# Token rows scattered straight into their expert's slot, without a token table, and two short static pieces

## The chip, the core and the metric

The kernel runs on one core of one Trainium2 chip. The metric is the device time of one execution, in microseconds (us); lower is better. Engines are called as in the profile: PE (TensorE, matmuls), DVE (VectorE), ACT (ScalarE), POOL (GpSimd), SP (SyncE, which here mostly issues DMAs). A q after the name (SPq) is the engine's own queue.

## The reference

A decayed linear attention ("retention") over 4 batches, 8 heads, 768 positions and head size 64 gives 3072 tokens of 512 features. They go through a mixture of 8 experts of which each token uses one:

```python
state = gamma * state + k[t] (x) v[t]            # per batch and head, 64 x 64
y[t]  = scale * q[t] @ state
x     = y as 3072 tokens x 512
logits = x @ w_gate + modality_bias[modality_id] # 8 experts
e_idx  = argmax(logits); gate_w = softmax(logits)[e_idx]
for e in range(8):                               # tokens whose e_idx is e
    out[mask] = gate_w[mask] * (relu(x[mask] @ w1[e]) @ w2[e])   # 512 -> 1024 -> 512
```

## The kernel before, in words

**Retention.** 24 tiles of 128 tokens (`NN`), six per batch. `retention(n)` is one tile, written as four steps with a `yield` behind each: state update (`state`, L200), scores of the next tile (`scores`, L139), projection of the previous tile (`tokens_out`, L180) and output heads (`heads_out`, L157). Loads run ahead on SP: keys and queries three tiles (`load_kq`, four buffers), values and token-wise keys two. `decay_v` (L130, POOL) scales the values; `decay_q` (L123, POOL) makes, once at the start, the six scaled versions of the table `dcq`, from which `heads_out` takes that of its tile. `tokens_out` multiplies by identity and gate weights in one matmul, so that a row of `xs` holds four groups of 128 features and 8 partial logits (`XW` = 544 floats, 2176 bytes); ACT copies it out of PSUM and stores it at the token's own place in `x_dram` (L190).

**Routing.** After every three tiles (a group, `GRP`) `route_a` finds the expert and the gate of 384 tokens and `route_b` the position: expert times 3072 plus the running number within the expert. `scatter` (L333) then writes, per tile, one row of 8 bytes per token (token number and gate) to that position of the table `tbl`, by an indirect DMA of POOL.

**Jobs.** A slot is 512 positions of one expert (`SLOT`); 48 slots could exist (`NCAND`). A job computes one slot: `ids_in` (L520, SP) reads the slot's 512 table rows, `gather` (L529) fetches their token rows from `x_dram` by four indirect DMAs of POOL, `flip` (L556) transposes them on PE and splits them into a high and a low part (ACT and DVE), `raw` and `cut` load the expert's weights and split them likewise, `first` and `second` are 96 matmuls each, and the result is scaled by the gate (ACT, L599) and scattered to `out` (POOL, L600). A job has 32 steps of 6 matmuls (`job_steps`); `hooks_of(k)` hangs work for the job itself and loads, transposes and cuts for the next one on these steps (a hook at q runs ahead of step 2q).

Two early jobs (`EARLY`: after groups 3 and 5) take a full slot each while retention goes on: from tile 14 on (`FIRST_JOB`), the steps of retention are put between job steps, two and one in turn. `early_a` to `early_e` choose the early slots. When all tokens are routed, `final_a` to `final_c` rank the slots left by size; four more jobs (`NLAST`) are laid out statically for the first four of them. SP reads slot and expert of each from a small list (`place`, `reg`). Where exactly five slots are left and the fifth has at most `TAIL` = 32 tokens, it goes through a short piece (`rest_in` to `rest_second`, L643 to L715), whose work is laid among the last two static jobs; otherwise the piece runs on the empty slot. All further slots go through a dynamic loop (L910), one pass each, which begins with loads and has no work of a neighbour to cover them.

**What sets the order.** PE, ACT, DVE and SP run in the order in which the program emits (`manual_schedule`); on POOL the pinned instructions keep it. `at(n, where, ...)` puts a piece of routing at a place of tile n: `top`, `st` (behind the state update), `sc` (behind the scores), `pr` (ahead of the projection), `tk` (behind it), `end`. Waits between engines come from the tiles' and DRAM tensors' uses; `disjoint` declares that scatters to other rows don't wait for each other.

Of the kernel before, what the change touches and what calls it, by code (L numbers as in the profile page):

```python
# [15 lines left out]
P = 128  # L16
# [4 lines left out]
NG = H // 2  # L21
# [12 lines left out]
TROWS = (NCAND + 1) * SLOT  # L34
# [9 lines left out]
C_ID, C_MASK, C_DEC, C_IOTA, C_GRP, C_FAC, C_END = 0, 128, 256, 304, 312, 313, 337  # L44
# [3 lines left out]
def kernel(  # L48
# [29 lines left out]
    x_dram = dr.tile([NT + P, XW], F32, name="x_dram")  # L78
    tbl = dr.tile([TROWS, 2], I32, name="tbl")
# [3 lines left out]
    dcq = cp.tile([P, NCH, NG, P], F32, name="dcq")  # L83
# [3 lines left out]
    fac = cst[:, C_FAC : C_FAC + NCH * NG].rearrange("p (c g) -> p c g", g=NG)  # L87
    iota_e = cst[:, C_IOTA : C_IOTA + NE]
# [6 lines left out]
    rows = cp.tile([P, NN, 2], I32, name="rows")  # L95
# [8 lines left out]
    kqs, kts, vts, vds, lg, mid = {}, {}, {}, {}, {}, {}  # L104
# [18 lines left out]
    def decay_q(c):  # L123
        pin(
            nc.gpsimd.tensor_tensor(
                dcq[:, c], dcq[:, 0], fac[:, c].unsqueeze(2).to_broadcast([P, NG, P]), op=ALU.mult
            )
        )
# [28 lines left out]
    def heads_out(n, a, vd, qv, s):  # L157
# [17 lines left out]
        for j in range(2):  # L175
            b = slice(2 * j, 2 * j + 2)
            nc.vector.tensor_tensor(yT[:, b], py[j], dcq[:, n % NCH, b], op=ALU.mult)  # L177
        return yT

    def tokens_out(n, yT):  # L180
        xs = wk.tile([P, NG, P + NE], F32, tag="xs", name=f"xs_{n}", bufs=3)
        for u in range(2):
# [7 lines left out]
        nc.scalar.dma_start(  # L190
            x_dram[n * P : (n + 1) * P, :].rearrange("t (g e) -> t g e", g=NG), xs
        )
        gr = n // GRP
        if n % GRP == 0:
            lg[gr] = sm.tile([P, GRP, NE], F32, tag="lg", name=f"lg_{gr}")
# [16 lines left out]


# [14 lines left out]
    def setup_rows():  # L228
        pin(nc.gpsimd.iota(rows[:, :, 0:1], [[P, NN], [0, 1]], base=0, channel_multiplier=1))
        fill["sent"] = me.tile([P, QW], F32, tag="raw", name="sent", bufs=4)  # L230
        sent = fill["sent"].bitcast(I32)[:, : TROWS // P * 2].rearrange("p (r w) -> p r w", w=2)
        pin(nc.gpsimd.memset(sent, 0))
        pin(nc.gpsimd.memset(sent[:, :, 0:1], NT))
        fill["zer"] = me.tile([P, QW], F32, tag="raw", name="zer", bufs=4)
        pin(nc.gpsimd.memset(fill["zer"][:, :XW], 0.0))

    def setup_stores():
        sent = fill["sent"].bitcast(I32)[:, : TROWS // P * 2].rearrange("p (r w) -> p r w", w=2)
        nc.sync.dma_start(tbl.rearrange("(p r) w -> p r w", p=P), sent)
        nc.sync.dma_start(x_dram[NT : NT + P, :], fill["zer"][:, :XW])  # L240

    def setup_room():
        jobs[0].xg = rows_room(jobs[0])
        for t in jobs[0].xg:
            pin(nc.gpsimd.memset(t, 0.0))
# [34 lines left out]
    def route_a(gr, part):  # L280
# [24 lines left out]
        else:  # L305
# [4 lines left out]
            nc.vector.reciprocal(rows.bitcast(F32)[:, tk, 1], den)  # L310
# [22 lines left out]
    def scatter(gr, which=range(GRP)):  # L333
        pos = mid[gr]
        for i in which:
            ins = nc.gpsimd.indirect_dma_start(  # L336
                out=tbl[:, :],
                out_offset=bass.IndirectOffsetOnAxis(ap=pos[:, i : i + 1], axis=0),
                in_=rows[:, gr * GRP + i, :],
                in_offset=None,  # L340
                bounds_check=NCAND * SLOT - 1,
# [676 lines left out]
```

## Time and profile before

| | us |
|---|---|
| median of 3 runs | 571.94 |
| lowest and highest run | 569.14, 573.87 |
| the profiled execution's own time | 571.58 |
| its span, first to last instruction | 569.8 |
| PE busy (matmul) | 497.5, 87% |
| DVE, ACT, POOL busy | 226.8, 166.7, 126.8 |
| DMA | 85.39 MB, mean 150 GB/s |

How to read it: the page cuts the span into 40 equal slices of 14.2 us and gives each engine's busy share in tenths (9 is 90% or more), the clock granted to PE in tenths of full speed, and the mean busy share of the 16 DMA engines with what they moved. A timeline row has start, duration, engine, line, operation, output <- inputs, count, and in square brackets how long the engine stood idle before it and what released it. A row of stretches has the stretch, its length, busy time and instruction count of PE, PEld (weight loads), DVE, ACT and POOL, then the granted clock, the DMA share and GB/s. A row of groups has busy time, mean duration in ns, and the idle time in front.

### The profile page before, as it was taken

Reading aid. Unit: us, or ns where it says so; the run is one execution under the profiler, and the core shown is the slowest. Engines: PE = TensorE matmul, PEld = TensorE weight load, DVE = VectorE, ACT = ScalarE, POOL = GpSimd, SP = SyncE. Lnnn points to the kernel's source line nnn. Section 1 sums busy time; section 2 is a strip of 40 time slices with the busy share of each in tenths; the row PEclk is TensorE's granted clock in tenths of the full one; section 3 lists DMA queues with packets and bytes.
Section 4 is the critical chain, followed back from the end, with each engine's and each line's share of the span. In section 5 each row is a group of like instructions: output and inputs, shape, how many; then the busy total and the mean of one; then the engine's idle time right before and its main releaser. Section 6 shows DMA issues by size and latency. Waiting matters only on the chain. (4 is left out here: it accounts for less than half of the span.)

```text
span 569.8 us, 8974 instructions
## 1 busy us (share of the span) xinstructions
PE 497.5 (87%) x3420; PEld 407.3 (71%) x3420; DVE 226.8 (40%) x460; ACT 166.7 (29%) x273; POOL 126.8 (22%) x132
## 2 busy tenths in 40 slices
PE   5997751999999999999999999999994799618995
PEld 5875640877887778888888888887883588506884
DVE  2764540776664455324425513622402440024400
ACT  1221120433332324334433424423313431024210
POOL 3553303222431322112022012120014100130011
PEclk9998785998999999999999999999998699956998
DMA  8989787296984436335335354862213500074000
GB/s 296 282 260 272 139 248 257 73 281 110 347 192 126 82 119 194 135 114 187 130 129 169 114 179 160 315 209 91 75 54 106 168 3 1 3 239 134 0 0 1
DMA packets 32838, 85.39 MB, mean 150 GB/s; under 512 B 7309, under 2 KB 7565, under 8 KB 32800
## 3 DMA queue, kind: packets, MB, share of 16 engines
q1 hardware_dynamic: 23104, 62.45, 37.2%
q0 software_dynamic: 5952, 15.31, 8.2%
q10 hardware_dynamic: 3744, 7.12, 3.4%
q8 instruction: 25, 0.41, 0.3%
q14 instruction: 13, 0.11, 0.1%
HBM read 71.38 MB, written 15.64 MB: 153 GB/s over the span
## 5 line engine op out<-in xcount | busy, mean ns | idle before, releaser
L553 DVE TENSOR_TENSOR lo_f<-raw_f,hi_f 128x1024 fp32r<-128x1024 f32 x32 | 39.2, 1225 | 49.3 <-ACT hi_f L551 44.5
L592 PE MATMUL o_f<-hi_f,hTh_f 128*128 128x512 f32 x128 | 50.5, 394 | 0.0
L574 PE MATMUL h_f<-xTh_f,hi_f 128*128 128x512 f32 x128 | 50.2, 393 | 0.0
L592 PE MATMUL o_f<-lo_f,hTh_f 128*128 128x512 f32 x128 | 49.9, 390 | 0.0
L592 PE MATMUL o_f<-hi_f,hTl_f 128*128 128x512 f32 x128 | 49.9, 390 | 0.0
L574 PE MATMUL h_f<-xTh_f,lo_f 128*128 128x512 f32 x128 | 49.9, 389 | 0.0
L574 PE MATMUL h_f<-xTl_f,hi_f 128*128 128x512 f32 x128 | 49.9, 389 | 0.0
L582 DVE SCALAR_TENSOR_TENSOR hTl_f<-h_f,hTh_f 128x512 fp32r<-128x512 f32 x32 | 21.9, 690 | 56.2 <-ACT hTh_f L581 54.2
L553 DVE TENSOR_TENSOR lo_dyn<-raw_dyn,hi_dyn 128x1024 fp32r<-128x1024 f32 x16 | 19.0, 1221 | 58.9 <-ACT hi_dyn L551 58.9
L151 DVE TENSOR_TENSOR a<-sc,cst 128x512 f32<-128x512 f32 x48 | 30.9, 684 | 27.5 <-PE sc L146 22.7
L600 POOL DMA_INDIRECT out_dram<-o_f,ids_f x16 | 15.8, 987 | 107.3 <-ACT o_f L599 96.1
L134 POOL TENSOR_TENSOR vd<-vt,cst 128x512 f32<-128x512 f32 x24 | 25.1, 1045 | 60.9 <-DMA vt<-in_qkv_dram 19.5
L146 PE MATMUL sc<-kq 64*128 64x128 f32 x384 | 32.9, 315 | 5.6 <-DMA kq<-in_qkv_dram 5.1
L559 PE MATMUL xp_dyn<-cst,xg_dyn 128*128 128x128 f32 x32 | 8.6, 432 | 31.0 <-DMA xg_dyn<-x_dram,ids_dyn 30.9
L146 PEld LDWEIGHTS sc<-kq 64*128 64x128 f32 x384 | 27.6, 215 | 10.2 <-DMA kq<-in_qkv_dram 5.3
L581 ACT ACTIVATE hTh_f<-h_f 128x512 fp32r<-128x512 f32 x32 | 19.1, 598 | 53.6 <-PE h_f L574 52.4
L551 ACT CAST hi_f<-raw_f 128x1024 fp32r<-128x1024 f32 x32 | 33.4, 1043 | 0.0
L336 POOL DMA_INDIRECT tbl<-rows,pos x24 | 24.6, 1026 | 36.0 <-DVE pos L330 14.5
L189 ACT COPY xs<-x 128x272 f32<-128x272 f32 x48 | 18.2, 385 | 48.9 <-PE x L185 38.2
L600 POOL DMA_INDIRECT out_dram<-o_dyn,ids_dyn x8 | 7.9, 990 | 101.0 <-ACT o_dyn L599 101.0
L185 PE MATMUL x<-wgt,yT 128*128 128x136 f32 x192 | 29.8, 301 | 0.5 <-DVE yT L177 0.5
L559 PEld LDWEIGHTS xp_dyn<-cst,xg_dyn 128*128 128x128 f32 x32 | 5.7, 217 | 33.9 <-DMA xg_dyn<-x_dram,ids_dyn 33.8
(192 smaller groups left out, 1052.9 us busy)
## 6 DMA issues: line engine op xcount, KB each, us to landing
raw_f<-in_w_dram SPq DMA_DIRECT2D x32, 512.0 KB
kq<-in_qkv_dram SPq DMA_DIRECT2D x23, 512.0 KB
raw_e<-in_w_dram SPq DMA_DIRECT2D x16, 512.0 KB
raw_dyn<-in_w_dram SPq DMA_DIRECT2D x16, 512.0 KB
x_dram<-xs ACTq DMA_DIRECT2D x24, 272.0 KB
vt<-in_qkv_dram SPq DMA_DIRECT2D x24, 256.0 KB
kt<-in_qkv_dram SPq DMA_DIRECT2D x20, 256.0 KB
rw<-in_w_dram SPq DMA_DIRECT2D x6, 512.0 KB
```

Of the source, the lines that this page charges most:

```text
L134: nc.gpsimd.tensor_tensor(vds[n], vv, dec[:, n % NCH].unsqueeze(2).to_broadcast([P, H, D]), op=ALU.mult)
L146: nc.tensor.matmul(pe[j][:, g * P : (g + 1) * P], kt[r, g], qt[r, g], start=True, stop=True, skip_group_check=True,)
L151: nc.vector.tensor_tensor(a[:, j], pe[j].rearrange("p (h t) -> p h t", t=P), mask.unsqueeze(1).to_broadcast([P, NG, P]), op=ALU.mult,)
L185: nc.tensor.matmul(px[:, g], yT[:, 2 * u + g], wgt[:, 2 * u + g], start=(g == 0), stop=(g == 1), skip_group_check=True,)
L336: ins = nc.gpsimd.indirect_dma_start(out=tbl[:, :], out_offset=bass.IndirectOffsetOnAxis(ap=pos[:, i : i + 1], axis=0), in_=rows[:, gr * G ...
L551: nc.scalar.copy(hi, t)
L553: nc.vector.tensor_tensor(lo, t, hi.bitcast(F32), op=ALU.subtract)
L574: nc.tensor.matmul(s.ph, s.w[1][f // 2][wi][:, o : o + P], s.xT[kc][a], start=(kc == 0 and k == 0), stop=(kc == KC - 1 and k == 2),)
L581: nc.scalar.activation(hi, s.ph, AF.Relu)
L582: nc.vector.scalar_tensor_tensor(lo, s.ph, 0.0, hi.bitcast(F32), op0=ALU.max, op1=ALU.subtract)
L592: nc.tensor.matmul(s.po, s.hT[f][a][:, hh * P : (hh + 1) * P], s.w[2][f // 2][wi][:, (f % 2) * DM : (f % 2 + 1) * DM], start=(f == 0 and k ...
L600: ins = nc.gpsimd.indirect_dma_start(out=out[:, :], out_offset=bass.IndirectOffsetOnAxis(ap=s.ids[:, hh, 0:1], axis=0), in_=o[:, :], in_of ...
```

## The change

Rows go straight to their place. `x_dram` and `tbl` are gone; `xsl` (8 experts x 3072 rows and one empty slot, 2176 bytes a row) takes their part. `tokens_out` stores nothing; the `xs` tiles are kept (four buffers, not three) until their group is routed. The gate is then written into the row (column 129, `reciprocal`, one operation per tile), the token's number too (column 128, an `iota` of POOL), and `scatter` sends the 128 rows of 2176 bytes by one indirect DMA of POOL. Routing of ordinary groups stands about one tile earlier. A job reads its slot by four plain SP loads (`rows_in`) and copies token numbers and gates into small tiles (`ids`, eight DVE copies).

Rows of a slot behind the last token have to hold "no token": after the last group `gaps_a` to `gaps_c` (DVE) work out where they are, and nine scatters (`gap`: one of single rows, eight, one per expert, of runs of four rows) fill them from a cleared tile. `rows_in` of the first static job waits for all of them.

Two short pieces (`NREST`) instead of one: the fifth and the sixth slot left over are taken by short pieces where they have 1 to 32 tokens and no more than six slots are left; the loop's end is lowered by as many. The first piece loads in the first static job and runs in the second; the other loads in the third and runs in the fourth.

Besides: `decay_q` makes a tile's scaled table when it is needed, by four ACT copies (none in the first tile of a batch); the four `kq` buffers become quarters of one tile `kqr`, whose space later holds the filler rows and a piece's weights; the list is picked by one matmul in place of four.

```diff
-            nc.scalar.dma_start(x_dram[n * P : (n + 1) * P, :]..., xs)
+    xsl = dr.tile([NONE + SLOT, XW], F32, name="xsl")
+    kqr = ld.tile([P, 4, 2, DM], F32, tag="kq", name="kqr", bufs=1)
...
     def load_kq(n, split=False):
-        t = kqs[n] = ld.tile([P, 2, DM], F32, tag="kq", name=f"kq_{n}", bufs=4)
+        t = kqs[n] = kqr[:, n % 4]
...
+    def decay_q(n):
+        c = n % NCH
+        if c == 0:
+            return dcq
+        t = wk.tile([P, NG, P], F32, tag="dq", name=f"dq_{n}")
+        for g in range(NG):
+            nc.scalar.activation(t[:, g], dcq[:, g], AF.Copy, scale=fac[:, c, g : g + 1])
+        return t
...
+    def scatter(gr, i):
+        n = gr * GRP + i
+        xs = xss.pop(n)
+        pin(nc.gpsimd.iota(xs.bitcast(I32)[:, 0, P : P + 1], [[0, 1]], base=n * P, channel_multiplier=1))
+        ins = nc.gpsimd.indirect_dma_start(
+            out=xsl[:, :],
+            out_offset=bass.IndirectOffsetOnAxis(ap=mid[gr][:, i : i + 1], axis=0),
+            in_=xs.rearrange("p g e -> p (g e)"), in_offset=None,
+            bounds_check=NONE - 1, oob_is_err=False,
+        )
+        disjoint(ins, "rows")
+        for tag in reads:
+            tc.declare_no_dep(ins.ins, group=tag, reason="rows of other tokens")
...
+    def final_d():
+        got = mid.pop("f")
+        slot, size, live = got[:, :NREST], got[:, NREST : 2 * NREST], got[:, 2 * NREST :]
+        short = small("short", [1, NREST])
+        nc.vector.tensor_scalar(short, size, float(TAIL), None, op0=ALU.is_le)
+        nc.vector.scalar_tensor_tensor(short, size, 0.0, short, op0=ALU.is_gt, op1=ALU.mult)
+        few = small("few", [1, 1])
+        nc.vector.tensor_scalar(few, live, float(NLAST + NREST), None, op0=ALU.is_le)
+        nc.vector.tensor_scalar(short, short, few, None, op0=ALU.mult)
...
+        nc.vector.tensor_tensor(ends[:, :1], live, nsh, op=ALU.subtract)
...
+    def gap(e):
+        one, pos = mid["g"]
+        n = 1 if e < 0 else RUN
+        ins = nc.gpsimd.indirect_dma_start(
+            out=xsl.rearrange("(r f) w -> r (f w)", f=n),
...
+            in_=fill["gap"][:, : n * XW], in_offset=None,
+            bounds_check=NONE // n - 1, oob_is_err=False,
+        )
...
-    def ids_in(s):
...
-    def gather(s):
...
+    def rows_in(s):
+        s.xg = [me.tile([P, XW], F32, tag=f"xg{hh}", name=f"xg{hh}_{s.tag}") for hh in range(HH)]
+        src = xsl[bass.ds(s.row, SLOT), :].rearrange("(h p) w -> h p w", p=P)
+        for hh in range(HH):
+            ins = nc.sync.dma_start(s.xg[hh], src[hh])
...
+    def ids(s):
+        for hh in range(HH):
+            t = s.xg[hh]
+            nc.vector.tensor_copy(s.tok[:, hh : hh + 1], t.bitcast(I32)[:, P : P + 1])
+            nc.vector.tensor_copy(s.gate[:, hh : hh + 1], t[:, P + 1 : P + 2])
...
-            at(t + 1, "st", route_a, g, 0)
-            at(t + 1, "end", route_a, g, 1)
-            at(t + 2, "st", route_a, g, 2)
-            at(t + 2, "sc", route_b, g)
+            at(t, "end", route_a, g, 0)
+            at(t + 1, "st", route_a, g, 1)
+            at(t + 1, "sc", route_a, g, 2)
+            at(t + 1, "sc", route_b, g)
             for i in range(GRP):
-                at(min(t + 2 + i, NN - 1), "pr", scatter, g, (i,))
+                at(min(t + 1 + i, NN - 1), "pr", scatter, g, i)
...
-    at(t + 1, "st", ids_in, e)
-    at(t + 1, "pr", gather, e)
+    at(t + 1, "pr", rows_in, e)
+    at(t + 2, "top", ids, e)
...
         route_b(NGRP - 1)
         final_b()
-        scatter(NGRP - 1)
+        scatter(NGRP - 1, 0)
+        yield PAUSE
+        gaps_a()
+        scatter(NGRP - 1, 1)
         yield PAUSE
         final_c()
+        gaps_b()
+        scatter(NGRP - 1, 2)
+        gaps_room()
+        yield PAUSE
+        final_d()
+        gaps_c()
+        for e in range(-1, NE):
+            gap(e)
+        place(jobs[NEARLY], lists["final"], 0, U)
...
-            on(5 if k == 0 else 3, ids_in, nxt)
-            on(6 if k == 0 else 5, gather, nxt)
+            on(6 if k == 0 else 5, rows_in, nxt)
+            on(8, ids, nxt)
...
+        for s, load_in, run_in in zip(rests, (2, 4), (3, 5)):
+            if k == load_in:
+                on(6, rest_in, s)
+                for i in range(8):
+                    on(6 + i, rest_load, s, 1 + i // 4, i % 4)
+            if k == run_in:
+                on(0, rest_flip, s)
+                on(2, rest_first, s)
+                on(4, rest_mid, s)
+                on(6, rest_second, s)
```

More of the change, by code (lines that the diff above doesn't have):

```diff
@@ L211, in state, with small @@
         return s
+    def small(nm, shape, dt=F32):
+        return cp.tile(shape, dt, name=nm)
     def setup_a():
@@ L228, in setup_rows @@
     def setup_rows():
[L229 to L235, printed above, removed]
-    def setup_stores():
[L238 to L245, printed above, removed]
+        none = fill["none"] = me.tile([P, QW], F32, tag="raw", name="none", bufs=4)[:, :XW]
+        pin(nc.gpsimd.memset(none, 0.0))
+        pin(nc.gpsimd.memset(none.bitcast(I32)[:, P : P + 1], NT))
+    def setup_stores():
+        for r in range(NONE, NONE + SLOT, P):
+            nc.sync.dma_start(xsl[r : r + P, :], fill["none"])
     mb = cp.tile([P, 2, NE], F32, name="mb")
@@ L309, in route_a @@
             nc.vector.tensor_scalar(den, den, 1e-9, None, op0=ALU.add)
-            nc.vector.reciprocal(rows.bitcast(F32)[:, tk, 1], den)
+            for i in range(GRP):
+                nc.vector.reciprocal(xss[gr * GRP + i][:, 0, P + 1 : P + 2], den[:, i : i + 1])
     def route_b(gr):
@@ L354 @@
     U = NLIST
-    def small(nm, shape, dt=F32):
-        return cp.tile(shape, dt, name=nm)
     lc, lists = {}, {}
@@ new lines, in gap @@
+    def gap(e):
[3 more added lines that the diff above has]
+            out=xsl.rearrange("(r f) w -> r (f w)", f=n),
+            out_offset=bass.IndirectOffsetOnAxis(
+                ap=one if e < 0 else pos[:, e : e + 1], axis=0
+            ),
+            in_=fill["gap"][:, : n * XW],
+            in_offset=None,
+            bounds_check=NONE // n - 1,
+            oob_is_err=False,
+        )
+        disjoint(ins, "rows")
@@ L630, in rest_load @@
         if k < 6:
[L631 to L632 removed]
+            if k < 4:
+                t = kqr[:, k].rearrange("p a b -> p (a b)")
+            else:
+                t = wk.tile([P, QW], F32, tag="a", name=f"rw{m}{i}", bufs=2)
             nc.sync.dma_start(t, src)
@@ L643, in rest_in @@
     def rest_in(s):
-        s.ids = me.tile([P, 2], I32, tag="rids", name="rids")
+        s.xg = wk.tile([P, XW], F32, tag="xs", name="rx", bufs=4)
         for g in range(4):
-            nc.sync.dma_start(s.ids[g * TAIL : (g + 1) * TAIL], tbl[bass.ds(s.row, TAIL), :])
-        s.xg = wk.tile([TAIL, XW], F32, tag="xs", name="rx", bufs=3)
-        nc.gpsimd.indirect_dma_start(
-            out=s.xg[:, :],
-            out_offset=None,
-            in_=x_dram[:, :],
-            in_offset=bass.IndirectOffsetOnAxis(ap=s.ids[:TAIL, 0:1], axis=0),
-            bounds_check=NT,
-            oob_is_err=False,
-        )
-        s.pos = me.tile([P, 1], I32, tag="rpos", name="rpos")
-        posf = me.tile([P, 1], F32, tag="rposf", name="rposf")
-        nc.vector.tensor_copy(posf, s.ids[:, 0:1])
-        nc.vector.scalar_tensor_tensor(posf, posf, 4.0, cst[:, C_GRP : C_GRP + 1], op0=ALU.mult, op1=ALU.add)
-        nc.vector.tensor_copy(s.pos, posf)
+            nc.sync.dma_start(s.xg[g * TAIL : (g + 1) * TAIL], xsl[bass.ds(s.row, TAIL), :])
     def rest_flip(s):
@@ L715, in rest_second @@
         disjoint(ins, "out_rows")
-    jobs = [Job(f"e{k}", g * GRP * P) for k, g in enumerate(EARLY)]
-    jobs += [Job(f"f{i}") for i in range(NLAST)]
-    rest = Job("r")
+    jobs = [Job(f"e{k}") for k in range(NEARLY)] + [Job(f"f{i}") for i in range(NLAST)]
+    rests = [Job(f"r{i}") for i in range(NREST)]
     hooks = {}
@@ L730, in run, with place_early @@
             fn(*args)
+    def place_early(k):
+        place(jobs[k], lists[k], 0, 1)
     def two(fn, s, m, ii):
@@ L917 @@
         ) * SLOT
-        ids_in(s)
-        gather(s)
+        rows_in(s)
+        ids(s)
         for kc in range(KC):
```

258 lines of the change are left out of this document (144 added, 114 removed).

## The prediction

> **What bounds the kernel now.** I read the page first: where does TensorE (PE) stop, and what do its clock and the DMA engines do there.
>
> ```profile
> span 569.8 us, 8974 instructions
> PE   5997751999999999999999999999994799618995
> PEclk9998785998999999999999999999998699956998
> DMA  8989787296984436335335354862213500074000
> ```
>
> A slice is 14.2 us. PE is full from slice 9 to 29, thin around slices 5 to 7, and ragged in the last ten. Stretches by stage, each row with the engines' busy time, granted clock, DMA share and GB/s:
>
> ```profile
> 80.00:94.00 14.00, 0.69 (x16) 0.58 (x16) 1.68 (x4) 1.54 (x3) 2.49 (x3) 0.56 0.94 364
> 225.00:267.00 42.00, 42.00 (x194) 34.89 (x193) 16.72 (x19) 15.54 (x22) 8.02 (x8) 1.00 0.41 140
> 434.00:499.00 65.00, 48.62 (x210) 39.16 (x208) 17.11 (x20) 17.93 (x25) 10.45 (x9) 0.89 0.17 54
> 499.00:565.00 66.00, 50.07 (x208) 40.33 (x208) 17.27 (x20) 17.43 (x24) 8.30 (x8) 0.82 0.25 81
> ```
>
> Three regimes: retention up to about 100 us, with a hole (80 to 94) in which PE does nothing and DMA runs at 0.94; static jobs, bound by PE at full clock; then two passes of the dynamic loop, each loading its weights and rows from cold. GpSimd's (POOL) timeline dates the passes: last static store, first gather of the loop, last store of the loop.
>
> ```profile
> 435.47 0.97 POOL L600 DMA_INDIRECT out_dram<-o_f,ids_f  x1 [4.46 <-ACT o_f L599]
> 437.10 1.60 POOL L532 DMA_INDIRECT xg_dyn<-x_dram,ids_dyn  x1 [0.66 <-issue]
> 564.71 0.97 POOL L600 DMA_INDIRECT out_dram<-o_dyn,ids_dyn  x1 [4.46 <-ACT o_dyn L599]
> ```
>
> **Term 1, the loop.** Worked out on the reference's own inputs, experts 0, 3 and 5 get 1567, 1502 and 3 tokens, the others none: eight live slots of 512, with 512, 512, 512, 31; 512, 512, 478; and 3 tokens. Two early jobs and four static ones take the six large; the loop's two passes are the slots of 31 and 3. The old short piece needs exactly five slots left (NLAST+1) and finds six, so it runs on the empty slot. The new test allows NLAST+2 = 6, and both sizes are at most TAIL = 32: both pieces become live, `ends[0]` is 6-2 = 4, and the loop from 4 to 4 runs no pass. From store to store that removes 564.71-435.47 = 129.2 us. What follows the last store (569.8-564.7 = 5.1) stays. Passing over the empty loop costs something like the 0.66 of idle before its first gather; I take +0.7, from 0 to 2.
>
> **Term 2, a second short piece** now runs in the second static job; the one in the last job was there. Its price is in ScalarE's (ACT) job-ending copies and PE's transposes for the next job:
>
> ```profile
> 340.59 0.69 ACT L599 ACTIVATE o_f<-o_f,ids_f 128x512 f32<-128x512 f32 x1 [3.82 <-issue]
> 385.98 0.69 ACT L599 ACTIVATE o_f<-o_f,ids_f 128x512 f32<-128x512 f32 x1 [3.82 <-issue]
> 434.51 0.69 ACT L599 ACTIVATE o_f<-o_f,ids_f 128x512 f32<-128x512 f32 x1 [4.75 <-PE o_f L592]
> ...
> 225.93 1.03 PE L559 MATMUL xp_f<-cst,xg_f 128*128 128x128 f32 x8
> 226.72 0.48 PE L592 MATMUL o_e<-hi_e,hTh_e 128*128 128x512 f32 x1
> ```
>
> A job without piece lasts 385.98-340.59 = 45.4, of which transposes are twice 226.72-225.93 = 1.6. The last job, with piece and without transposes, lasts 48.5: the piece costs 48.5-43.8 = +4.7. Its 4 MB of weights load during the first static job, where DMA share is 0.41.
>
> **Term 3, retention and the hole.** The table takes rows of 8 bytes. What comes after three such scatters, and after a scatter of 2 KB rows (280 to 286):
>
> ```profile
> 34.84 1.16 POOL L336 DMA_INDIRECT tbl<-rows,pos  x1 [3.15 <-DVE lg L196]
> ...
> 33.00:39.00 6.00, 5.96 (x91) 5.03 (x89) 2.48 (x8) 1.14 (x3) 3.54 (x4) 1.00 0.92 314
> 39.00:46.00 7.00, 4.99 (x76) 4.04 (x76) 6.52 (x19) 1.83 (x6) 3.61 (x6) 1.00 0.70 41
> 57.00:63.00 6.00, 4.73 (x77) 4.05 (x77) 4.00 (x14) 1.55 (x5) 1.71 (x2) 1.00 0.48 21
> 280.00:286.00 6.00, 6.00 (x28) 4.99 (x27) 1.26 (x2) 2.12 (x3) 1.58 (x2) 1.00 0.38 131
> ...
> 40.31 1.16 PE L146 MATMUL sc<-kq 64*128 64x128 f32 x16
> 47.88 1.12 PE L205 MATMUL st<-vd,kt 128*64 128x64 f32 x16 [3.66 <-DMA kt<-in_qkv_dram]
> 48.94 2.08 PE L146 MATMUL sc<-kq 64*128 64x128 f32 x16
> ```
>
> For some 6 us the DMA engines stay busy (0.70, 0.48) and move 41 or 21 GB/s; before, 0.92 gave 314. The 2 KB scatter has no such shadow (0.38, 131). The changed kernel scatters rows of 2176 bytes only, so I take the shadow away. At 47.88 that is worth the wait of 3.66, and the two groups after it that ran at half clock: 2.08 for 1.16 and about as much on the 1.12, some 1.4: -5.1. Routing now starts a tile earlier, in the order that early groups use; there PE waits for `oh`, first row below. Two groups before the first job take that order: +2.5. Now the hole:
>
> ```profile
> 62.57 0.19 PE L315 MATMUL rk<-oh,upper 128*128 128x24 bf16 x1 [1.27 <-DVE oh L298]
> ...
> 75.53 2.71 SPq L546 DMA_DIRECT2D raw_e<-in_w_dram  x4
> 82.92 0.34 SPq L522 DMA_DIRECT2D ids_e<-tbl  x1
> ...
> 90.90 1.08 POOL L532 DMA_INDIRECT xg_e<-x_dram,ids_e  x1 [14.86 <-DMA kq<-in_qkv_dram]
> ...
> 94.64 0.44 PE L559 MATMUL xp_e<-cst,xg_e 128*128 128x128 f32 x1 [13.67 <-DMA xg_e<-x_dram,ids_e]
> 98.70 0.48 PE L559 MATMUL xp_e<-cst,xg_e 128*128 128x128 f32 x1 [0.86 <-DMA xg_e<-x_dram,ids_e]
> 99.11 2.08 PE L146 MATMUL sc<-kq 64*128 64x128 f32 x16
> ...
> 78.00:91.00 13.00, 1.38 (x30) 1.02 (x26) 2.71 (x7) 1.63 (x4) 0.10 (x1) 0.65 1.02 392
> ...
> 500.69 1.60 DMA ids_dyn<-tbl
> ```
>
> Today SyncE (SP) queues 2.1 MB of weights at 75.53 and 1 MB for retention, then the ids; these land when that backlog is through (90.9); only then POOL gathers four times, the first landing 3.7 us after its start, the last block at 98.7. In the change, four plain row loads (1.11 MB) stand about where the ids stood. With weights at 75.5-5.1+2.5 = 72.9, the queue holds 2.1+1.05+1.11 = 4.3 MB, at 392 GB/s 10.9 us: 83.8, plus 1.6 to land: 85.4. With 0.8 of transposes `sc` starts at 86.2, not 99.11: **-12.9** for all of term 3. Bounds: 0 (the loads keep PE waiting as long as now) and -23 (waiting 94.64-13.67 to 99.11 and the 5.1 vanish). I stay between, as the bytes ahead of the rows remain. From 106 on PE is busy with the early job; I take 0 there, from -2 to +3.
>
> **Term 4, the filler rows.** Before the first static job may read its slot, nine new scatters must land, behind twelve small DVE operations that stand after the DVE's second half of a job step:
>
> ```profile
> 207.71 0.69 DVE L582 SCALAR_TENSOR_TENSOR hTl_e<-h_e,hTh_e 128x512 fp32r<-128x512 f32 x1 [2.55 <-issue]
> 205.21 0.97 POOL L336 DMA_INDIRECT tbl<-rows,pos  x1 [0.30 <-issue]
> L336 POOL DMA_INDIRECT tbl<-rows,pos x24: 966/978/1747, 34.8 to 205.2; - x24
> ```
>
> In today's clock: DVE free at 208.4, twelve operations of some 0.18 (the copy of 128x1 further down takes 0.15): 210.6. POOL issues one per 0.97+0.30 = 1.27. The last that writes much (expert 5, seventh) starts at 218.2, 1.1 MB, lands at 218.2+3.7+2.1 (0.83 MB more at 392) = 224.0; the ninth starts at 220.8 and lands at 224.5. SP waits there; behind it stand weights not needed for another job half. Then four row loads: 1.11 MB at 392 is 2.8, plus 1.6 to land, plus issue 0.4: 229.3. The transposes stand at 225.93 and cannot wait unseen: 3.4 us, and 1.7 for the half clock that followed the 3.66 wait: **+5.1**. From 0 (landings overlap better) to +12 (each issue as long as the slowest, 1.75).
>
> Here a rule of the Trainium skill speaks against the change: SBUF — State Buffer, section "SBUF: two separate sides", says that a DMA issued from GpSimd stalls while VectorE runs an operation that takes the shared port pair, since descriptors can't be written, and its subsection "A bandwidth-pool intuition that's wrong" gives about 3100 ns for a DMA of 620. By that, nine issues would cost 9 x 2.5 = 22 us more, an estimate, and the sum would be 462. The trace agrees only in kind: at worst 1.75 for 0.98.
>
> **Costed at nothing.** Rows for ACT, DVE and a load's wait:
>
> ```profile
> L189 ACT COPY xs<-x 128x272 f32<-128x272 f32 x48 | 18.2, 385 | 48.9 <-PE x L185 38.2 <-issue 4.7 <-DMA x_dram<-xs 4.0
> L706 ACT ACTIVATE ro<-ro,rids 128x128 f32<-128x128 f32 x1 | 0.4, 368 | 1.3 <-PE ro L698 1.3
> L659 DVE CAST rposf<-rids 128x1 f32<-128x1 int32 x1 | 0.2, 153 | 6.0 <-issue 6.0
> 82.81 1.04 ACT L551 CAST hi_e<-raw_e 128x1024 fp32r<-128x1024 f32 x1 [4.72 <-DMA raw_e<-in_w_dram]
> ```
>
> (a) Scaling `dcq` moves from five POOL operations to four ACT copies in each of 20 tiles: 4 x 0.37 = 1.5 us a tile, under ACT's 48.9 us of waiting before the `xs` copies; without that cover 29 us. They stand between the state copy and the `xs` copies, and their result is wanted only at the tile's end. (b) Token and gate copies: 8 x 0.15 = 1.2 us of DVE a job, in a DVE busy 16.7 of 42; they stand before the transposes' split, so they delay it only if the rows are late. (c) The `xs` rows leave by POOL after routing instead of by ACT at once. A buffer is wanted again four tiles later, about one tile after its scatter is issued; a scatter takes 3.7 to land and a tile about 5, so ACT may wait 0 to 2 us, three times before the hole: 0, up to +6; PE has eight banks of slack. (d) In the static jobs four SP loads replace four gathers at the same half step. The transposes follow 3 of 16 steps later, 8.5 us; the loads need 2.8 + 1.6. At this stretch's 140 GB/s they would need 7.9 + 1.6: 1 us late in each of three jobs. (e) The clearing of the filler tile and the row-number fills (POOL, idle 34 of 42 us), and 0.6 MB more of empty rows at 26 us: 1.6 us at 392 GB/s, if nothing covers it.
>
> **The sum** against the profiled execution, 571.6 (span 569.8 and 1.8 around it): 571.6 - 129.2 + 0.7 + 4.7 - 12.9 + 5.1 = **440.0**. The median of the runs is 571.9, 0.4 above it; 440 stands for both. Its own range is 429 to 452: term 3's lower bound and term 1's to one side (-10, -1), to the other term 4's +7 and half of (c), (d), (e).
>
> **Rivals.**
>
> Hole stays. The four row loads come last in the same SP queue, the weights drain as slowly as now, and retention waits on scatters: term 3 gives 0 and (c) its middle: 440+12.9+3 = 456. For it: the hole's DMA share is 1.02 already. Against it: 6 us of shadow go, and the gathers' serial 98.70-90.90 = 7.8.
>
> Slow fillers. Each of the nine issues takes 1.75, and the loads behind them lose their slack: 440+7+5 = 452. For it: twelve DVE operations just before; against it: the median of 0.98. By the figure of the Trainium skill's page SBUF — State Buffer it would be 462.
>
> Deeper gain. Row loads hide entirely, term 3 reaches -23: 430.
>
> The loop stays. If one of the two small slots doesn't qualify, one pass of some 65 us remains (434 to 499): 505. If neither does, both remain: 569, no change. Against it: 31 fits under 32 by one row and 6 equals the limit, but both are met.
>
> Slower: serial loads. `kqr` becomes one tile in place of four buffers. If dependencies are kept for the whole tile, each tile's load must wait until the last reader of the other three quarters is through, and the next scores wait for the load. A 512 KB load issued at 75.53 was used at 82.81: 7.3 us, in 23 tiles 168: 440+168 = 608. It decides from (571.6-440)/23 = 5.7 us a tile. For it: the change of the tile alone; against it: `dcq` and `wgt`, written and read in parts today, show no wait of that kind among the longest; which is weak.
>
> **How the numbers follow.** The forecast 0.70; hole stays 0.10; slow fillers 0.07; deeper gain 0.05; one pass left 0.03; both left 0.02; serial loads 0.03. Faster by over 1%: 0.95; within 1% (569 is): 0.02; slower: 0.03. The runs before differ by 0.4% from their median, so 1% is about what a measurement tells from no change. The range, 427 to 459, holds the forecast with its bounds, the deeper gain and the first two rivals, and leaves out the loop's and the serial loads' cases, 0.08, and some tails.
>
> **What would show it.** Right: no `dyn` tile in the trace; the last store of the static jobs some 5 to 6 us before the end; two groups `rxp`, `rh`, `ro` of PE work, the job that got the second one 4.7 longer; no stretch in the first 80 us with DMA share over 0.45 at under 60 GB/s; the first job's transposes at about 85 and the `sc` after them at 86; before the first static job's transposes a PE wait of 3 to 4 us on rows, behind fillers that POOL issues 1.3 apart. Wrong: any `dyn` row; DMA still choked after row scatters; PE waits on `kq` in every tile; ACT waits on scatters for more than 2 us at a time; PE waits before the transposes of later static jobs. The sum is wrong in size if the hole is longer than 9 us or the filler wait longer than 6.

## The result, and the profile after

Four runs of the changed kernel gave a median of 452.35 us (451.86 to 453.46), four of the kernel before 572.58: a ratio of 0.791, 95% interval 0.787 to 0.795. The profiled execution took 452.26, its span 450.3. The forecast was 440.0, the range 427 to 459. The page's head for the changed kernel:

```profile
span 450.3 us, 8319 instructions
PE   4995959299799999999479999999999999999994
PEclk9998988879989999999869999999999999999998
DMA  8988655938548832334562347952534279810011
```

A slice is now 11.3 us. The ragged last quarter is gone; PE is full from slice 11 on, but for two slices (19 and 20, about 214 to 236) that were full before. The stretches that were shown of before, in the kernel after (columns as before):

```profile
80.00:94.00 14.00, 5.25 (x47) 3.76 (x44) 5.36 (x22) 3.19 (x8) 1.12 (x2) 0.71 0.97 353
225.00:267.00 42.00, 39.32 (x169) 32.01 (x170) 13.66 (x22) 13.03 (x18) 3.89 (x4) 0.91 0.39 134
```

Between 80 and 94 PE works 5.25 us where it worked 0.69; from 225 on it has lost 2.7 us and a tenth of its clock. Now the way through the kernel by four marks: the `sc` behind the first transposes (99.11 before), the last output copy of the second early job (249.80 before), the last one of the last static job (434.51 before), and the end. PE's timeline:

```profile
88.84 1.07 PE L642 MATMUL xp_e<-cst,xg_e 128*128 128x128 f32 x2 [8.18 <-DMA xg_e<-xsl]
...
91.21 2.08 PE L159 MATMUL sc<-kqr 64*128 64x128 f32 x16
```

ACT's timeline, the last output copy of the second early job and of each static job:

```profile
254.30 0.69 ACT L682 ACTIVATE o_e<-o_e,gate_e 128x512 f32<-128x512 f32 x1 [3.82 <-issue]
...
299.78 0.69 ACT L682 ACTIVATE o_f<-o_f,gate_f 128x512 f32<-128x512 f32 x1 [3.81 <-issue]
...
350.26 0.69 ACT L682 ACTIVATE o_f<-o_f,gate_f 128x512 f32<-128x512 f32 x1 [3.82 <-issue]
...
395.74 0.69 ACT L682 ACTIVATE o_f<-o_f,gate_f 128x512 f32<-128x512 f32 x1 [3.81 <-issue]
...
444.45 0.69 ACT L682 ACTIVATE o_f<-o_f,gate_f 128x512 f32<-128x512 f32 x1 [4.75 <-PEq L1005]
```

DVE's timeline after (its half of the job step behind which the fillers' last positions are worked out, 207.71 before), and ACT's timeline before:

```profile
200.65 0.69 DVE L665 SCALAR_TENSOR_TENSOR hTl_e<-h_e,hTh_e 128x512 fp32r<-128x512 f32 x1 [0.44 <-ACT hTh_e L664]
```

```profile
249.80 0.69 ACT L599 ACTIVATE o_e<-o_e,ids_e 128x512 f32<-128x512 f32 x1 [3.82 <-issue]
```

The hole ends 7.9 us earlier (99.11 to 91.21), and 7.1 of that reach DVE's half step in the second early job (207.71 to 200.65). That job's end is 4.5 us *later* than before (249.80 to 254.30): 11.6 us are lost between. The four static jobs take 45.48, 50.48, 45.48 and 48.71: the second, which got the new piece, is 5.0 longer than its neighbours. Behind the last copy stand 5.9 us and no loop. So 569.8 - 129.2 (loop) - 0.2 (passing over it, and the end) - 7.1 + 11.6 + 5.4 (static jobs, 190.15 against 184.71 in sum) = 450.3. Two losses want a cause. ACT's timeline in retention shows the first:

```profile
39.85 0.67 ACT L205 COPY xs<-x 128x272 f32<-128x272 f32 x2 [9.52 <-DMA xsl<-xs,pos]
43.72 0.67 ACT L205 COPY xs<-x 128x272 f32<-128x272 f32 x2 [2.91 <-DMA xsl<-xs,pos]
...
56.89 0.68 ACT L205 COPY xs<-x 128x272 f32<-128x272 f32 x2 [4.11 <-DMA xsl<-xs,pos]
```

ACT waits 16.5 us for scatters that still read an `xs` buffer. The chain that ended last shows the second, ahead of the first static job (start, length, what):

```profile
201.69 2.40 DVE short L516
...
205.10 0.47 POOL xsl L583
...
217.43 5.04 DMA xsl<-kqr,run_pos
222.68 0.33 SPq L612
...
224.45 4.59 DMA xg_f<-xsl
229.08 1.33 PE xp_f L642 x5
```

One DVE operation of two numbers takes 2.4 us; nine filler issues run from 205.10 to 218.4, two of them twice as long as the others; the last lands at 222.5; then the rows are loaded. PE's waits on them, from the waits view of 205 to 233:

```profile
PE xp_f L642 <- DMA xg_f<-xsl: 8.6, 4, 6.3
```

### The profile page after: what moved, and what is told of

Its sections match the earlier page's. It is cut to its first block, busy times and chain, and to the rows that moved or that the text cites. A ratio compares the mean times of both kernels' runs of the same rounds, so it can differ in the third digit from the quotient of the medians.

```text
span 450.3 us, 8319 instructions
## 1 busy us (share of the span) xinstructions
PE 405.9 (90%) x3104; PEld 331.3 (74%) x3104; DVE 201.0 (45%) x509; ACT 156.4 (35%) x309; POOL 92.3 (20%) x116
## 4 chain that ended last, share of the span: by engine, by line
PE 51%; issue 13%; DVE 3%; POOL 2%; DMA 2%; ACT 1%; POOLq 0%; SPq 0%; DVEq 0%; ACTq 0%
PE h_f L657 15%; PE o_f L675 14%; PE o_e L675 9%; PE h_e L657 3%; PE x L201 2%; PE xp_f L642 2%; PE y L183 2%; PE sc L159 1%; POOL xsl L583 1%; DMA xsl<-kqr,run_pos 1%; DMA xg_f<-xsl 1%; DVE lo_e L636 1%; POOL out_dram L683 1%; PE y L177 1%; PE st L215 1%
## 5 line engine op out<-in xcount | busy, mean ns | idle before, releaser
L683 POOL DMA_INDIRECT out_dram<-o_f,tok_f x16 | 15.5, 969 | 132.8 <-ACT o_f L682 113.8
L345 POOL DMA_INDIRECT xsl<-xs,pos x24 | 25.6, 1066 | 58.6 <-DVE xTl_e L648 9.1
L201 PE MATMUL x<-wgt,yT 128*128 128x136 f32 x192 | 30.9, 309 | 5.5 <-DVE yT L190 5.5
L159 PE MATMUL sc<-kqr 64*128 64x128 f32 x384 | 30.8, 304 | 5.0 <-DMA kqr<-in_qkv_dram 4.9
L201 PEld LDWEIGHTS x<-wgt,yT 128*128 128x128 f32 x192 | 27.3, 209 | 7.4 <-DVE yT L190 3.4
L159 PEld LDWEIGHTS sc<-kqr 64*128 64x128 f32 x384 | 25.9, 205 | 9.3 <-DMA kqr<-in_qkv_dram 5.1
L682 ACT ACTIVATE o_f<-o_f,gate_f 128x512 f32<-128x512 f32 x16 | 11.0, 688 | 59.9 <-issue 34.1
L657 PEld LDWEIGHTS h_f<-xTh_f,hi_f 128*128 128x128 f32 x128 | 24.0, 188 | 6.2 <-issue 1.2
L183 PE MATMUL y<-a,vd 128*64 128x128 f32 x384 | 28.4, 294 | 0.0
```

The costliest lines, as they stand in the source:

```text
L159: nc.tensor.matmul(pe[j][:, g * P : (g + 1) * P], kt[r, g], qt[r, g], start=True, stop=True, skip_group_check=True,)
L183: nc.tensor.matmul(py[j][g % 2 * D : (g % 2 + 1) * D, g // 2], vd[:, 2 * g + j], a[:, j, g], start=(s is None and g < 2), stop=(g >= 2), s ...
L201: nc.tensor.matmul(px[:, g], yT[:, 2 * u + g], wgt[:, 2 * u + g], start=(g == 0), stop=(g == 1), skip_group_check=True,)
L345: ins = nc.gpsimd.indirect_dma_start(out=xsl[:, :], out_offset=bass.IndirectOffsetOnAxis(ap=mid[gr][:, i : i + 1], axis=0), in_=xs.rearran ...
L657: nc.tensor.matmul(s.ph, s.w[1][f // 2][wi][:, o : o + P], s.xT[kc][a], start=(kc == 0 and k == 0), stop=(kc == KC - 1 and k == 2),)
L683: ins = nc.gpsimd.indirect_dma_start(out=out[:, :], out_offset=bass.IndirectOffsetOnAxis(ap=s.tok[:, hh : hh + 1], axis=0), in_=o[:, :], i ...
```

## The experiments

My theory: the forecast missed 12 us by two sizes, the wait for `xs` buffers that I had costed at nothing, and the fillers' chain. Rivals are named in each expectation. Runs 1 to 4, 5 to 8 and 9 to 12 shared a chip each, with 7 runs of the kernel before on it (568.66, 570.14 and 570.25). Ratios are to those.

**Six buffers.**

```diff
-        xs = xss[n] = wk.tile(..., tag="xs", name=f"xs_{n}", bufs=4)
+        xs = xss[n] = wk.tile(..., tag="xs", name=f"xs_{n}", bufs=6)
```

> Edit: six x buffers instead of four, nothing else. Theory R (the ring): the three waits of ScalarE for a buffer (16.5 us together, longest 9.5) come from reuse after four tiles, while a group of three has to be routed and scattered first. With six they go, the first transposes of the first job come 5 to 7 us earlier (first copy after them from 91.2 to about 85 to 86), and the end about as much: 445 to 447.5 us against 452.3. Theory S (the first scatter): what is late is the first scatter, at 33.8, because it is ordered after the four stores of empty rows (their last packet ends at 32.3), and VectorE's and TensorE's waits behind GpSimd stay with six buffers; then the gain is 2 to 3 us (449.5 to 450.5). Theory N: TensorE's waits in these tiles have other causes and only ScalarE's idle time goes: within 1 us of 452.3.

444.54 us (444.21 to 444.83), ratio 0.782, 0.778 to 0.786. Timelines of ACT (the copies that waited longest before) and of PE:

```profile
33.23 0.85 ACT L205 COPY xs<-x 128x272 f32<-128x272 f32 x2 [1.82 <-PE x L201]
39.33 0.85 ACT L205 COPY xs<-x 128x272 f32<-128x272 f32 x2 [1.37 <-PE x L201]
```

```profile
83.50 2.08 PE L159 MATMUL sc<-kqr 64*128 64x128 f32 x16
```

The waits on scatters are gone and `sc` comes at 83.50. Theory R holds. Its gain is kept to the end: the second early job ends at 246.41 instead of 254.30.

**The first scatter freed** of its order behind the stores of empty rows.

```diff
-        for tag in reads:
+        for tag in ["none_rows"] + reads:     # the four stores are put in group none_rows
```

> Edit: the scatters are declared independent of the four stores of empty rows (they write other rows); four x buffers as in the changed kernel. Under R the first scatter is issued at about 30.5 to 31 instead of 33.8, the longest wait of ScalarE falls from 9.5 to 6 to 7 us, the other two stay, and the end moves by 1 to 2.5 us: 450 to 451.5. Under S nearly all of the loss goes: 446 to 448. If the first scatter is still issued at 33 to 34, the stores are not what it waits for, and the time stays at 452 to 453.

453.09 us (449.40 to 454.52), ratio 0.796, 0.790 to 0.802: no gain. Timelines of POOL and of ACT:

```profile
31.23 1.17 POOL L346 DMA_INDIRECT xsl<-xs,pos  x1 [4.56 <-DVE yT L190]
```

```profile
40.27 0.67 ACT L205 COPY xs<-x 128x272 f32<-128x272 f32 x2 [9.33 <-DMA xsl<-xs,pos]
```

The first scatter was indeed held by the stores (33.82 in the changed kernel, 31.23 here), but ACT's wait is as long. In this trace the first scatter's packets begin only at 36.4, 5.1 us behind the start of its issue: the DMA engines were busy (share 0.90 from 31 to 36, 0.99 from 36 to 40), and the earlier issue did not land earlier. Theory S falls, and so does the 1 to 2.5 us that R gave this run.

**Four filler issues instead of nine.**

```diff
-        for e in range(-1, NE):
+        for e in (-1, 0, 3, 5):
```

> Edit: filler issues only for the single rows and for the three experts that have tokens in this data (0, 3 and 5); the other five would write nothing here, since their counts are 0. All bytes that were written are still written. Theory P (the serial issues set it): five issues fewer, 1.27 to 1.3 us each, so the rows of the first static job land 6 to 6.5 us earlier, the 8.6 us of TensorE's waits before its transposes fall to 2 to 3, the half-clock stretch behind them shrinks, and the end comes 6 to 8 us earlier: 444 to 446.5. Theory Q (the writes set it: rows of 8.7 kB still on their way): the last landing stays near 222 and the time within 2 us: 450 to 452.3. Theory C (the stretch to the first static job is long because of the clock, not because of the wait): waits go, and the time falls by less than 2 us all the same.

446.81 us (445.23 to 450.74), ratio 0.787, 0.781 to 0.794. SP's timeline, and PE's waits from 205 to 233:

```profile
216.60 2.09 SPq L612 DMA_DIRECT2D xg_f<-xsl  x4
```

```profile
PE xp_f L642 <- DMA xg_f<-xsl: 3.2, 4, 1.9
```

PE's wait falls from 8.6 to 3.2 as theory P said. From the `sc` behind the first transposes to the last output copy of the second early job the changed kernel takes 163.1 us in each of two profiles, this one 158.0, 5.1 less. At the end the medians give 3 to 5.5, but the intervals overlap. Both are below P's 6 to 8: PE's clock still drops to half for 6.8 us beside the shorter waits, as it did for 10.2 beside the long ones.

**One pass of the loop kept.**

```diff
         nc.vector.tensor_scalar(short, short, few, None, op0=ALU.mult)
+        nc.vector.memset(short[:, :1], 0.0)
```

> Edit: the piece of 31 rows is no longer counted as short, so that one pass of the loop at the end does it; the static piece in its place runs on empty rows. My price of one pass is 64.6 us (129.2 for two in the kernel before): 452.3 + 64.6 = 516.9, between 515 and 519. Rival: passes do not cost the same, most of the loop's cost is in entering it or in the first pass (cold loads and a cold clock): then one pass is 70 us or more, 522 and above; or the two passes overlapped little and one costs under 60: below 512.

508.19 us, one run: 8.7 under the expected value, in the range of the second rival. ACT's timeline (last copy of the static jobs, and of the pass), and PE's waits from 440 to 505:

```profile
442.33 0.69 ACT L683 ACTIVATE o_f<-o_f,gate_f 128x512 f32<-128x512 f32 x1 [4.76 <-PE o_f L676]
...
500.39 0.69 ACT L683 ACTIVATE o_dyn<-o_dyn,gate_dyn 128x512 f32<-128x512 f32 x1 [4.75 <-PE o_dyn L676]
```

```profile
PE xp_dyn L643 <- DMA xg_dyn<-xsl: 5.2, 2, 4.7
```

The pass costs 58.1. In the kernel before, the same distances are 59.4 and 69.8 (434.51 to 493.91 to 563.75), by ACT's timeline:

```profile
493.91 0.69 ACT L599 ACTIVATE o_dyn<-o_dyn,ids_dyn 128x512 f32<-128x512 f32 x1 [4.75 <-PE o_dyn L592]
```

```profile
563.75 0.69 ACT L599 ACTIVATE o_dyn<-o_dyn,ids_dyn 128x512 f32<-128x512 f32 x1 [4.75 <-PE o_dyn L592]
```

There PE waited 11.2 and 19.7 us for rows fetched by way of the table. So the 129.2 removed was two unlike passes, and not twice the price of one pass now. Against the old first pass the new one saves 1.3 only, though PE waits 6 less for rows; how much plain slot reads save is not shown by one run with one pass. In this run the static jobs also ended 2.1 earlier than in the first profile.

**The changed kernel once more**, on the chip of the next three.

> The changed kernel itself once more, as a mark on this chip for the other runs: 452.3, between 449 and 454 (the kernel before gave 572.6 and 568.7 on the two occasions so far).

450.04 us (449.06 to 452.00), ratio 0.791, 0.786 to 0.795. Its profile has `sc` at 87.89, 3.3 earlier than the first one: two profiles of one kernel differ by that much in retention.

**No clearing of the filler source.**

```diff
         t = fill["gap"] = ...
-        pin(nc.gpsimd.memset(t, 0.0))
         tn = t.bitcast(I32)...[:, :, P : P + 1]
         pin(nc.gpsimd.memset(tn, NT))
```

> Edit: the filler's source is not cleared to zero on GpSimd any more (1.94 us); only its four token words are set, and the x part of the filler rows holds old query and key values instead of zeros. Theory M (the clearing slows VectorE): in the changed kernel VectorE's step at 201.7 took 2.39 us while GpSimd cleared, and the first filler waited for VectorE until 205.10. Without the clearing VectorE's positions are done 2 us earlier, all nine issues and the rows shift by 2 us, and the end comes 1.5 to 2.5 us earlier. Rival: the step is long by itself (its releases), GpSimd only idles longer, and the end stays within 0.7 us.

445.64 us (443.47 to 446.39), ratio 0.781, 0.777 to 0.786: 4.4 less than its neighbour, twice what I gave it. DVE's timeline:

```profile
199.55 0.40 DVE L516 TENSOR_SCALAR short<-short,few 1x2 f32<-1x2 f32 x1
...
201.15 0.17 DVE L576 TENSOR_TENSOR run_pos<-run,far_r 128x8 int32<-128x8 f32 x1
```

The same operation took 2.39 in the changed kernel (2.38 in its second profile) while GpSimd's clearing ran; without the clearing, 0.40. POOL's timeline in the changed kernel:

```profile
202.12 1.94 POOL L529 MEMSET kqr<- 128x2176 f32 x1
```

The Trainium skill, SBUF — State Buffer, section "SBUF: two separate sides", describes the port pair that VectorE and GpSimd share as an exclusive lock that one of them holds for its whole instruction while the other waits; of VectorE's operations it counts those in a 2-port mode or with two SBUF inputs. This run agrees that the operation waited for GpSimd: in the changed kernel its row starts at 201.69, while GpSimd still issues the last `x` scatter (to 202.11), and ends at 204.08, 0.02 behind the clearing; without the clearing it ends with that issue (199.95 and 199.96). But other small operations of DVE beside the same issue took 0.15, so which of them wait is not shown. Counted from the start of the last `x` scatter, the positions come 2.0 earlier (2.35 for 4.37), but the row loads 6.1 (15.33 for 21.42). The rest: the single rows' filler, whose positions are ready before, now goes out while the others are still computed, and the last filler packet ends 0.1 us behind the last issue (213.09, issue over at 212.99) and not 3.2 behind it (218.29, 215.05).

**Fewer filler bytes.**

```diff
+        d = small("d", [P, NE])                       # end - up, in runs of four rows
+        nc.vector.tensor_tensor(d, end, up, op=ALU.subtract)
+        nc.vector.tensor_scalar(d, d, 120.0, 120.0, op0=ALU.is_ge, op1=ALU.mult)
+        nc.vector.tensor_tensor(end, end, d, op=ALU.subtract)
```

> Edit: of a slot with at most 32 rows in use only the 32 rows that a short piece reads are filled; left out are the other filler rows of such slots, which only a pass of the loop would read (none is made here). Nine issues as before, but 2.1 MB less written. Theory P (serial issues): the two long issues (2.03 and 1.95 against 0.97) shrink to 1.0, the last issue ends at 216.3 instead of 218.4, and the rest of the gain is the last landing; the end comes 2 to 4 us earlier. Theory Q (the bytes set it): the rows of the first static job could start as soon as the last issue lands, TensorE's 8.6 us fall below 4, and the end comes 5 to 7 us earlier. Rival: neither, the end stays within 1 us.

449.26 us (448.48 to 451.24), ratio 0.790, 0.785 to 0.794: not to be told from its neighbour's 450.04, so nothing of the 2 to 7 us is shown. In the profile PE's wait fell to 5.8. And the long issues stayed, which my reason for them (the bytes) does not allow. POOL's timeline, the second and third filler issues:

```profile
203.83 1.55 POOL L587 DMA_INDIRECT xsl<-kqr,run_pos  x1 [0.30 <-issue]
205.68 2.02 POOL L587 DMA_INDIRECT xsl<-kqr,run_pos  x1 [0.31 <-issue]
```

DVE's timeline at the same time (`lo_e` is the low part of a weight block, cut for the job under way):

```profile
203.31 1.22 DVE L640 TENSOR_TENSOR lo_e<-raw_e,hi_e 128x1024 fp32r<-128x1024 f32 x1
...
205.64 1.21 DVE L640 TENSOR_TENSOR lo_e<-raw_e,hi_e 128x1024 fp32r<-128x1024 f32 x1
```

So it is not the bytes but DVE: both issues start while DVE cuts weights, and both end 0.85 us behind that operation (204.53 to 205.38, 206.85 to 207.70); the third long one (1.50, at 210.55) ends 0.84 behind the next. The two long issues of the changed kernel (2.03 at 207.78, 1.95 at 212.64) end 0.84 behind cuts as well. The traces show this everywhere: of 914 indirect issues of GpSimd in the 14 profiles 46 took over 1.2 us, and every one of them starts during a cut of DVE (or with it) and ends 0.83 to 0.93 behind the cut. Of 61 that start more than 0.13 us ahead of a cut's end, only two were not held, and these start within 0.03 us of the cut's start. It is a reading of times: no run moved the cuts.

**Five buffers, five issues, no clearing** (`bufs=5`, `RUN = 8`, one issue for two experts).

> A version meant to be kept, from what the first four runs showed: five x buffers, filler runs of eight rows so that one issue serves two experts (five issues instead of nine, the same rows filled), no clearing of their source (the x part holds old query and key values). The ring gives 5 to 7.5 us (six gave 7.5), four issues fewer 3.5 to 5, the clearing 1.5 to 2: 438 to 442, below the changed kernel and the 444.5 of six buffers alone. Rival: five buffers are too few, since a scatter takes 6 us to land and the fifth tile after it comes before that: ScalarE still waits 3 us or more in one or two places, and the gain is 3 us less: 442 to 445. Second rival: rows of 17 kB take the DMA engines longer than the issues save: no gain from the fillers, 445 to 447.

442.05 us (439.65 to 442.81), ratio 0.775, 0.770 to 0.779. That is at the upper edge of the expected range, where the rival's begins; but the rival's wait did not come: no wait of ACT on a scatter is left, so five buffers suffice for that. `sc` comes at 86.67, 2.4 to 3.2 later than with six in one profile each; whether the fifth buffer is the reason is not shown.

**Six buffers, no clearing.**

> The two single edits that paid most, together: six x buffers and no clearing of the filler source (nine issues, runs of four rows). They act in different stages (retention, and the way to the first static job), so they should add: against the changed kernel's 450 to 452, 5 to 7.5 us for the buffers and 4.4 for the clearing: 439 to 442. Rival: with retention earlier the wait for the rows only grows back (TensorE gets there earlier, the fillers not): 443 to 445.

439.87 us (437.99 to 442.86), ratio 0.770, 0.767 to 0.774. The two gains add at the end; `sc` at 84.31. PE still waits 5.5 us for the first static job's rows, where the run without clearing alone had 3.5, so 2 us of that wait did grow back. This has the lowest median of all, not clear of the 442.05; its interval lies wholly below that of the changed kernel (0.786 to 0.795).

**The table's writes brought back**, 8 bytes a row, and the same with 512.

```diff
+        if gr == NGRP - 1:
+            return
+        ins = nc.gpsimd.indirect_dma_start(
+            out=tb[:, :],                               # [NONE, 2] or [NONE, 128]
+            out_offset=bass.IndirectOffsetOnAxis(ap=mid[gr][:, i : i + 1], axis=0),
+            in_=cst[:, C_IOTA : C_IOTA + 2],            # or ident
...
+        disjoint(ins, "tb_rows")
```

> Work added to the six-buffer kernel (444.5): after each scatter of x rows, in all groups but the last, a second scatter of 128 rows of 8 bytes to the same places of a table that nobody reads, from a constant. It brings back the writes of the old token table without its waits. Theory W (8-byte writes hold up the other transfers, the reason I gave for 5.1 us of the retention term): packets of the loads slow down for 5 to 6 us after each group, loads of q, k and v come late, the first copy after the first transposes comes 3 to 6 us later and the end 3 to 7 us later: 447.5 to 451.5. Theory I (GpSimd's issues cost, not the writes): as with rows of 512 bytes, 1.3 us a tile on GpSimd, at most 2 us at the end. Theory H (hidden): 444 to 445.5.

> The same added scatters, with rows of 512 bytes instead of 8 (64 times the bytes, the same number of rows and issues). Theory W: no slow packets behind them, 444 to 446.5, at least 2.5 us below the run with 8 bytes. Theory I: the same time as with 8 bytes, within 1 us. Theory B (bytes count): slower than with 8 bytes.

458.57 us (454.44 to 460.57), ratio 0.802, 0.797 to 0.807, with 8 bytes; 459.54 (457.77 to 460.09), ratio 0.806, 0.804 to 0.809, with 512. That is 14 and 15 us above the 444.54 of six buffers, which ran on another chip (11 and 14 by the ratios). The stretch 51 to 58 (columns as in the stretches above) of the one and of the other:

```profile
51.00:58.00 7.00, 5.55 (x84) 4.61 (x80) 3.26 (x9) 2.46 (x9) 4.87 (x6) 1.00 0.91 65
```

```profile
51.00:58.00 7.00, 6.53 (x104) 5.34 (x102) 2.71 (x8) 2.65 (x9) 4.72 (x6) 1.00 0.87 242
```

The shadow is real and belongs to the 8-byte rows: a DMA share of 0.91 moves 65 GB/s, against 242 at 0.87. Counted from the traces between 30 and 80 us, packets of 2 to 5 kB that took over 0.7 us: 146 in the kernel before, 37 in the changed one, 134 with 8-byte rows added, 45 with 512. The Trainium skill (DMA: Bandwidth & Descriptors, Specifications) has transfers under 512 bytes done as read, modify and write, which fits the line between the two. But it is hardly on the path: `sc` comes at 91.56 with 8 bytes and at 90.12 with 512 (84.31 without either and without the clearing, same chip), less apart than two profiles of one kernel; only a wait of PE for `kt`, 2.8 us, comes back with 8 bytes and not with 512. What costs is what both runs add alike: issues in GpSimd's queue, 1.3 us each, of 128 rows each (the first two even go out ahead of the first `x` scatter). That is theory I in kind, at six to seven times the 2 us that I gave it; W's price falls. By which wait the issues reach PE is shown in part only: ahead of the hole the longest new one in both is PE's for DVE's `pick`, 3.9 and 3.8 us (at most 0.4 with six buffers), and PE waits for no scaled values (`vd`).

**ScalarE's table scaling left out.**

```diff
         c = n % NCH
-        if c == 0:
-            return dcq
+        return dcq
```

> Left out of the six-buffer kernel: ScalarE's 80 copies of 0.39 us that scale the query decay per chunk (the unscaled table is used for all chunks, so later chunks come out with another scale). My step costed them at nothing in the changed kernel. Theory: ScalarE is 35% busy, the copies lie in its idle time, and the end stays within 1 us of 444.5. Rival: in the tiles before the first job, where four copies (1.6 us) go in front of the x copies of the same tile on ScalarE, they delay the routing and the hole: 441 to 443.

765.48 us, which says nothing: other values route the tokens otherwise, to more slots, and the loop runs. Only the part ahead of the first job can be compared (same chip, 84.31 with the scaling); PE's timeline:

```profile
82.08 2.08 PE L158 MATMUL sc<-kqr 64*128 64x128 f32 x16
```

2.2 us earlier (1.4 than the other profile of six buffers, 83.50; the two differ by 0.8). One profile, so likely 1 to 2 us: the rival is nearer than the theory.

## Why the prediction was right or wrong, point by point

The forecast's span was 438.2 (440.0 less 1.8), the profile's is 450.3. Of these 12.1 us term 3 holds 5.0, the early jobs behind it 0.8, term 4 6.5 and term 2 0.7; term 1 gives back 0.9. The time lies in the range, just above the 452 of the sum's own bounds, and the ratio is near because term 1 alone is 129 us. Two of the forecast's own signs of being wrong came: ACT waits on scatters of more than 2 us, and a filler wait of more than 6.

**Term 1**, the loop: right. No `dyn` instruction in the trace, 129.2 less, and passing over cost nothing where I took 0.7.

**Term 2**, the second piece: right in kind, +5.0 in the job that got it, +5.4 over the four jobs, for 4.7.

**Term 3**: the step that failed is (c), costed at "0, up to +6": "A buffer is wanted again four tiles later, about one tile after its scatter is issued; a scatter takes 3.7 to land". The trace after has ACT want the fifth buffer at 30.3, 3.5 us *before* the first scatter is issued (33.82), since a group of three is routed only when its third tile is through, and the scatter then needs 6.0 to land among retention's loads (the 3.7 was a gather's, from 90.90 to 94.64 before). The longest wait is 9.5 and PE has no cover for it: it waits 5.3 us for `yT` ahead of the hole, and not at all with six buffers. With six buffers `sc` comes at 83.5 and 84.3; in the six profiles with four buffers and the changed kernel's waits, at 87.9 to 91.2, 89.6 in the mean. So (c) cost about 5.7: its upper end. Without it, the rest of term 3 would have given 99.1-83.9 = 15.2 for the 12.9 forecast.

Within that rest, the shadow was shown, its price of 5.1 was not: 8-byte rows cost 1.4 more than 512-byte rows at the hole, in one profile each. PE's last work ahead of the hole ends at 73.2 with six buffers and at 80.97 before, 7.8 earlier where I had -5.1+2.5. Up to there PE does 899 matmuls in both; it is busy for 65.2 us and idle for 15.8 before, busy for 60.7 and idle for 12.5 with six buffers (62.5 and 10.9 in the profile that also lacks the clearing). So 3.2 to 4.9 of it are waits, and 2.7 to 4.5 are shorter busy time, most of it less work at half clock (10.2 us between 20 us and the hole before, 3.4 and 6.8 with six buffers). The waits for `kt`, 5.3 before, are gone. Which change freed these loads (no 8-byte rows, one store fewer on ACT's queue, fewer packets) was not taken apart. The hole itself was 8.2 us of waiting, as the last paragraph of the forecast allowed.

**Term 4**: forecast +5.1, measured +11.6, the upper end of its range. By its own steps, in before's clock: positions ready at 212.6, not 210.6 (the DVE operation locked by the clearing); the last issue at 224.5, not 220.8 (that delay, and two issues of 2.0 instead of 0.97, both started during a cut of DVE); landed at 229.5, not 224.5 (5.0 instead of 3.7); rows there at 236.1, not 229.3 (6.6 instead of 4.8). Dropping the clearing gave back 4.4, dropping five issues 3 to 5.5 by the medians. The rival "slow fillers" was the nearest to the time, by chance: its mechanism, every issue at 1.75, did not come, and seven of nine took 0.96 to 1.10. The 22 us that the prediction estimated from the Trainium skill's page SBUF — State Buffer did not come either: two issues were held, by 1 us each. More was lost the other way round, by GpSimd's clearing holding up VectorE (4.4 at the end).

**Costed at nothing**: (a) is probably not nothing but 1 to 2 us at the hole. (b), (d), (e): the later static jobs show no PE wait on rows (45.48 twice, 45.4 before), so they were hidden; of (e) only the clearing was not, as said.

**The other rivals.** The hole did not stay, both pieces qualified, and PE waits for `kqr` only once, 4.9 us at the start (5.1 before). "Deeper gain" fell short: the hole still waits 8 us.

**What stays open**: which change freed retention's loads, by which waits added issues of GpSimd reach PE, and why most small DVE operations beside an issue don't wait while that one did.

## What to carry to other kernels

When a store moves from right behind its producer to behind a later decision, count the buffers from the time when the buffer is wanted to the time when the decision's transfer has *landed under load*, and not in tiles: here two more buffers (4 kB of each partition) were worth 5 to 8 us. When new small work lands in front of a dependent load, write out its whole chain, the clearing of its source included, and look for what each link shares with its neighbour. And an in-order queue that feeds the critical engine (GpSimd, with 1.3 us an issue) has a price per issue that hardly depends on bytes (8 or 512 a row here).

## What the runs showed of the hardware that was not expected

A VectorE operation on two numbers took 2.38 to 2.39 us beside a 1.94 us clearing on GpSimd, 0.40 without it. In the other direction, an indirect issue of GpSimd that starts during DVE's 1.2 us cut of weights ended 0.83 to 0.93 us behind the cut (but for two of 61) and took up to 2.13 us; all others took at most 1.17. Scatters of 128 rows of 8 bytes made 134 packets of 2 to 5 kB slow (up to 4.1 us each), the same with 512 bytes 45 (up to 2.3), hardly more than without (40 on that chip). A scatter issued 2.6 us earlier into busy DMA engines landed no earlier. PE's clock was at half for 6.8 us beside waits of 3.2 us in sum, none over 1.9, and for 10.2 beside 8.6: two and three times 3.4.
